# A redrawn order list and bank string for a fused delta-rule attention and MLP kernel

## The chip, the cores and the metric

The kernel runs on one core of one Trainium2 chip. The metric is the time of the device in microseconds (us), taken as the median of several runs. Each run starts the program once.

The core has five engines that run side by side, each through its own list of instructions: PE (matrix products, written to PSUM, which has eight banks of 128 x 512 float32), DVE and ACT (both read PSUM and SBUF; ACT also has the function tables), POOL (element work in SBUF, and the start of the weight transfers) and SP (starts of transfers). An engine executes its list strictly in order, and each instruction may wait for semaphores that other engines or transfers raise.

## The reference

The input is `q`, `k`, `v` of 4 batches x 8 heads x 768 positions x 48 dimensions, a factor `beta` for each position, and two weight matrices of 384 x 2048 and 2048 x 384. First comes a recurrence along the positions, then a dense block on its result:

```python
k_n = k / (norm(k) + 1e-6)
for t in range(S):                       # S = 768, one 48 x 48 state per head
    y[:, :, t] = einsum('bhd,bhde->bhe', q[:, :, t], state)
    v_old = einsum('bhde,bhd->bhe', state, k_n[:, :, t])
    state = state + b_t * einsum('bhd,bhe->bhde', k_n[:, :, t], v_t - v_old)
x = y, with the 8 heads x 48 side by side, 3072 rows of 384
h = x @ w_in
g = 0.5 * h * (1 + tanh(sqrt(2/pi) * (h + 0.044715 * h**3)))
out = g @ w_out
```

## The kernel before

**Chunks.** The recurrence is worked in 12 chunks (c0 to c11) of 64 positions for all 32 heads at once. Inside a chunk the dependence of one position on those before it is a triangular system; its inverse is built from 16 x 16 blocks: the small diagonal blocks are solved element by element (on DVE for c0, on POOL for c1 and for the later pairs c2/c3, c4/c5 and so on), and the larger block-triangular parts by Horner steps of matrix products (`inverse`, `factors`, `apply`). Chunks are then tied together by the state alone: `state(c)` computes R = K S - V, then U = T R, then the new state S from K and U, and the chunk's output x from S, Q, U.

**MLP.** When a chunk (c0 to c3) or a pair of chunks (from c4) has its x, `mlp` runs on these rows: the first product (m1, in units of one PSUM bank, each emptied by ACT with the gelu into `gT`), then the second (m2, eight tiles of `gT` at a time), whose result goes to `osb` and to DRAM. m1 needs all of `w_in` (six transfers on POOL, `g77` to `g82`), m2 the four parts of `w_out` (`g83` to `g86`). The MLP is the bulk of the PE's work and serves to fill its time between the short steps of the chunks.

**The order.** The program is first described as 1306 steps, numbered in the order in which the code makes them; each step says what it reads and writes, so its dependencies are known. A step is one or many instructions (a matrix step 2 to 64 products). Which engine runs a step, and in which order each engine runs its steps, is not computed: it stands written out in the string `ORDER`, where `p66` means "step 66 on PE", `v` is DVE, `a` ACT, `g` POOL and `s` SP (`a` and `s` also for transfers that these engines start). `w4.0` means four filler products of 512 columns into bank 0, which nobody reads. `BANK` gives for each PSUM tile the first of its banks. `Plan.schedule` (line 137) reads both, checks that no step stands ahead of one that it depends on, and makes a step that takes a bank wait for all users of the tile that had the bank before. `Plan.emit` (line 168) writes the five instruction lists with their waits. The position in `ORDER` matters only among steps of the same engine.

**Steps that the prediction names:**

| step | what it is |
|---|---|
| a23, a24 | masks mB0, mE0 (ACT) |
| 97, 99 | copy of the two halves of c0's transposed K out of PSUM into KQT (line 704) |
| 106, 107 | copy of the transposed Q of c0 and of c1 (line 673) |
| 112 | 1/norm of c1; 7, 49, 50, 51, 0: memsets (Kn, S3, the two EB halves, the filler's operand `wz`) |
| 75 | nbT, a transpose of beta (line 587); 71: bM of c0 |
| 158 to 180 | DVE's solve for c0 (177, 178: its last two large ops; 179, 180: into TB) |
| 187, 188 | c0's TT halves out of TB, four instructions each (line 934 on ACT, 935 on DVE) |
| 194, 196 ... 213 | PE steps of `apply` for c0, in two halves y = 0, 1 |
| 199, 201, 204, 207 | its results WB out of PSUM; 210, 214: U; 211, 215: the same for U3 |
| 217, 218, 219 | new state S after c0: product, copies S1 and S3 |
| 220 to 224 | output of c0: products, then copies into x |
| 135, 127 | K of c3 and c2; 136, 128: their transposes on PE; 137, 129: copies into KQT |
| 393, 394 ("own") | 64 small products each: diagonal blocks for c2 and c3; 396: their transpose Tt on DVE, which the POOL solve of c2/c3 starts from (397 to 426) |
| 316, 317 | for c1: K S on PE, and R on DVE (line 1162) |
| 312, 314; 313, 315 | c1's ET products and their copies |
| 318, 320, 322 ... 337 | PE steps of `apply` for c1; 319, 321: DI copies; 343 to 347: c1's output |
| 380, 381, 382, 383 | norms of c5 (square, sum) and of c4/c5 (square root) |
| 229, 231 ... 243 | m1 units of the first MLP tile; 230 ... 244: their gelu copies |
| 139, 140 | cast of Q for c2/c3 (POOL, ACT); 153 to 156: the loads of q for c4/c5, into the same buffer; 257, 258: casts of these; 259: transposes; 118 to 121: the loads of q for c2/c3 |
| 151, 152 | loads of k for c5 |
| 386, 389 | transposes of K for c4 and c5 |
| 443 | first Horner product of c2; 473, 474, 477, 478: c2's U product, its copy, and two products behind it |
| 1250, 1251 | last output product, last copy into x |
| 1298 to 1303 | the last m2 products; 1304, 1300: copies of their results into osb; 1293, 1297, 1305, 1301: transfers to DRAM |

Many DVE and ACT instructions are recorded under lines 252 and 257 (`f_tt`, `f_cp`) and 261 (`f_act`), PE's under 268 (`f_mms`) and transfers under 276 (`f_dma`), since these helpers make them.

## Time and profile before

| | us |
|---|---|
| median of 3 runs (lowest, highest) | 245.21 (243.59, 246.71) |
| the profiled execution, whole | 245.94 |
| its span from first to last instruction | 244.2 |
| PE busy in the span | 205.9 (84%) |
| DVE, ACT, POOL busy | 159.5, 154.4, 126.6 |
| instruction blocks (queue q8) | 35 transfers, 0.57 MB |

All times in the views are counted from the start of the span. The profiled execution took 1.7 us more than its span, and lies 0.7 us above the median. A busy time of PE counts a product from its issue to its modelled end, so neighbours overlap.

### The profile page before, as it was taken

How to read it: one execution, taken by the hardware profiler on the slowest of the kernel's cores; microseconds unless marked ns; L12 is line 12 of the kernel's file. 1: busy time of each engine (PE TensorE's matmuls, PEld its weight loads, DVE VectorE, ACT ScalarE, POOL GpSimd, SP SyncE). 2: the span in 40 equal slices, each digit the busy share in tenths (PEclk: the TensorE clock that was granted, in tenths of full speed). 3: DMA queues.
4: the chain of work that ended last, by engine and by line, in shares of the span. 5: the costliest groups of instructions: out<-in, count | busy, mean ns of one | idle time of the engine just before them, and what ended most of it. 6: DMA issues, size and time to landing. Idle time of an engine off the chain costs nothing.

```text
span 244.2 us, 10249 instructions
## 1 busy us (share of the span) xinstructions
PE 205.9 (84%) x4536; PEld 143.3 (59%) x4554; DVE 159.5 (65%) x300; ACT 154.4 (63%) x299; POOL 126.6 (52%) x267
## 2 busy tenths in 40 slices
PE   2144686498898889999998999999999799899995
PEld 2123565287755776877875666666566465555562
DVE  4689789459799979989799763893587453220000
ACT  0748635359699979973788979778631367105810
POOL 3566888189795886878504988358833000000000
PEclk9999999999999999999999999999999999999999
DMA  7979999795679247674435510044203202000122
GB/s 125 179 118 179 157 210 168 95 173 123 124 160 172 42 73 152 137 178 81 58 85 105 128 44 3 22 111 91 56 3 75 71 3 99 3 19 32 44 86 97
DMA packets 64780, 23.69 MB, mean 97 GB/s; under 512 B 53600, under 2 KB 63840, under 8 KB 64736
## 3 DMA queue, kind: packets, MB, share of 16 engines
q1 hardware_dynamic: 57984, 14.67, 34.7%
q0 software_dynamic: 1056, 3.15, 7.7%
q10 hardware_dynamic: 5696, 5.23, 7.1%
q8 instruction: 35, 0.57, 1.0%
q14 instruction: 9, 0.07, 0.1%
HBM read 20.64 MB, written 4.72 MB: 104 GB/s over the span
## 4 chain that ended last, share of the span: by engine, by line
PE 48%; DVE 18%; ACT 16%; DMA 7%; issue 5%; SPq 3%; ACTq 1%
PE ps L268 44%; SPq L276 3%; DMA x<-x 3%; DVE DT L752 2%; PE ps L697 2%; ACT KQT L261 2%; DMA qf<-in_q_dram 2%; DVE Tt L906 2%; DMA kf<-in_k_dram 2%; DVE EB L252 2%; ACT gT L261 2%; ACT EB L1099 1%; ACTq L276 1%; ACT Tt L736 1%; ACT x L261 1%
## 5 line engine op out<-in xcount | busy, mean ns | idle before, releaser
L268 PE MATMUL ps<-x,W 128*128 128x256 bf16 (+1 forms) x367 | 67.9, 325 | 5.0 <-DMA x<-x 2.1
L268 PE MATMUL ps<-W,gT 128*128 128x384 bf16 x384 | 66.8, 326 | 0.0
L261 ACT ACTIVATE gT<-ps 128x512 bf16<-128x512 f32 x96 | 53.0, 601 | 20.2 <-PE ps L268 19.5
L268 PEld LDWEIGHTS ps<-x,W 128*128 128x128 bf16 x384 | 39.2, 115 | 20.1 <-ACT gT L261 2.3
L268 PEld LDWEIGHTS ps<-W,gT 128*128 128x128 bf16 x384 | 35.9, 98 | 23.0
L795 POOL TENSOR_TENSOR Yf<-Yf,tmp 128x28 f32<-128x28 f32 (+13 forms) x84 | 30.1, 358 | 6.1
L252 DVE TENSOR_TENSOR TT<-ps,DI 128x768 bf16<-128x768 f32 (+2 forms) x30 | 20.6, 688 | 18.2 <-PE ps L268 18.0
L792 POOL TENSOR_TENSOR tmp<-Yf 128x28 f32<-128x28 f32 (+13 forms) x84 | 28.4, 338 | 6.0
L261 ACT ACTIVATE KQT<-ps 128x1024 bf16<-128x1024 bf16 (+1 forms) x16 | 15.5, 967 | 8.5 <-PE ps L697 6.8
L268 PE MATMUL ps<-KQT 48*64 48x128 bf16 (+1 forms) x640 | 12.7, 219 | 9.2 <-ACT KQT L261 5.7
L1029 POOL TENSOR_TENSOR DI<-TB,mB 128x384 bf16<-128x384 bf16 x14 | 13.0, 936 | 13.8 <-DVE TB L839 7.1
L261 ACT ACTIVATE osb<-ps 128x384 f32<-128x384 f32 x17 | 8.4, 493 | 17.9 <-PE ps L268 17.8
L257 DVE COPY osb<-ps 128x384 f32<-128x384 f32 x7 | 3.9, 551 | 24.1 <-PE ps L268 24.1
L752 DVE TENSOR_TENSOR DT<-ps,mD 128x512 bf16<-128x512 f32 x24 | 15.9, 680 | 2.7 <-ACT G L261 2.5
L268 PEld LDWEIGHTS ps<-KQT 48*64 48x64 bf16 (+1 forms) x640 | 9.2, 108 | 12.1 <-ACT KQT L261 7.2
L697 PE MATMUL ps<-identB,Kn 128*128 128x128 bf16 x96 | 8.9, 250 | 7.7 <-DVE Kn L252 6.0
L261 ACT ACTIVATE G<-ps 128x512 bf16<-128x512 f32 x24 | 13.9, 594 | 1.2 <-PE ps L268 0.8
L261 ACT ACTIVATE x<-ps 128x1024 bf16<-128x1024 f32 (+3 forms) x12 | 9.9, 829 | 7.2 <-PE ps L268 7.0
L261 ACT ACTIVATE U<-ps 128x768 bf16<-128x768 f32 (+1 forms) x9 | 7.0, 778 | 9.5 <-PE ps L268 9.5
L252 DVE TENSOR_TENSOR EB<-ps,mE 64x768 bf16<-64x768 f32 x13 | 12.3, 949 | 0.8 <-PE ps L268 0.5
L252 DVE TENSOR_TENSOR R<-ps,vf 128x768 bf16<-128x768 f32 x11 | 10.5, 952 | 3.0 <-PE ps L268 2.9
L252 DVE TENSOR_TENSOR S<-ps,S 128x768 bf16<-128x768 f32 x10 | 9.5, 951 | 4.4 <-PE ps L268 4.3
(144 smaller groups left out, 351.5 us busy)
## 6 DMA issues: line engine op xcount, KB each, us to landing
qf<-in_q_dram SPq DMA_DIRECT2D x24, 192.0 KB, 4.1
kf<-in_k_dram SPq DMA_DIRECT2D x23, 192.0 KB, 5.2
vf<-in_v_dram SPq DMA_DIRECT2D x40, 96.0 KB, 3.6
out_dram<-osb ACTq DMA_DIRECT2D x16, 192.0 KB, 1.9
W<-in_moe_w_out_dram POOLq DMA_DIRECT2D x4, 384.0 KB, 8.5
out_dram<-osb ACTq DMA_DIRECT2D x16, 96.0 KB, 2.8
vf<-in_v_dram SPq DMA_DIRECT2D x4, 192.0 KB, 5.7
W<-in_moe_w_in_dram POOLq DMA_DIRECT2D x2, 384.0 KB, 8.5
```

What stands on the lines that cost most here:

```text
L252: return lambda e: e.tensor_tensor(out() if callable(out) else out, a() if callable(a) else a, b() if callable(b) else b, op)
L257: return lambda e: e.tensor_copy(out, a() if callable(a) else a)
L261: return lambda e: e.activation(out, a() if callable(a) else a, func)
L268: ins = t.matmul(out, lhsT, rhs, start=st, stop=sp_, skip_group_check=skip)
L276: return lambda e: e.dma_start(out, a)
L697: ins = e.transpose(tb()[:, m, :], t[:, 2 * m:2 * m + 2, :].rearrange("p h d -> p (h d)"), identB[:, :])
L736: "act": lambda e: e.activation(X, gs_(0), ACT.Copy, scale=mH[:, 0:1]),
L752: op(d_ps(512), {"dve": lambda e: e.tensor_tensor(dv, gview(1)(), md, ALU.mult)}, reads=[h] + MD, writes=[dn])
L792: sop(nb * s * w, lambda e, s=s, w=w, tv=tv: e.tensor_tensor(tv, yf[:, :, s:s + 1, 0:s].to_broadcast([128, nb, w, s]), Yv()[:, :, s + 1:16 ...
L795: sop(nb * s * w, lambda e, s=s, tv=tv: e.tensor_tensor(Yv()[:, :, s + 1:16, 0:s], Yv()[:, :, s + 1:16, 0:s], tv, ALU.add), [YN, TN], [YN])
L906: op({"dve": 1.2 if early else 1.93}, {"dve": lambda e: e.transpose(Tt[j][:, 0:1024].rearrange("q (x y) -> q x y", y=32), own_view())}, re ...
L1029: return e.tensor_tensor(o_.rearrange("q p (b j) -> q p b j", j=16), i_.unsqueeze(2).to_broadcast([128, n_, 3, 16]), mB[:, 16 - 16 * w:64 ...
```

## The change

The string `ORDER` and the string `BANK` are replaced by others. The same 1306 steps are in it, each once, and the fillers are now `w6.3` (six products into bank 3) where `w4.0` stood elsewhere. No line of code outside the two strings changes: sizes, dependencies, loads and arithmetic are the same. 106 steps change their engine: 37 go from ACT to DVE and 36 from DVE to ACT, 10 from DVE to POOL and 8 from POOL to DVE, 13 transfers change between ACT and SP, one step goes from POOL to ACT and one back. DVE ends with 287 entries instead of 288, ACT with 310 instead of 312, POOL with 259 instead of 257, SP with 124 instead of 123, PE with the same 326. On every engine the order is another: at the start of the list the POOL's weight transfers `g77` to `g85` come earlier among its solve for c1, with `g86`, which stood first, after them; SP's loads are interleaved in another way; and PE runs the fillers ahead of step 393 rather than behind step 318. The diff, cut to the first 21 lines and the last two of each list, and the bank strings:

```diff
--- before.py
+++ after.py
@@ -17,68 +17,68 @@
 ORDER = """
-s54 v42 a55 g16 v1 v48 g21 v49 s52 g11 a53 s56 v46 v6 v47 v36 g12 g50 s57 g13 p66 g18 v68 v9 s59 v15 v3 v10 v37 v38
-v39 v5 v67 a87 g89 s63 v88 g17 v90 g19 v4 v40 v75 a2 s62 a91 a92 v93 s58 a108 v94 g95 s60 v41 p96 v69 s61 v109 g20 a97
-p98 s116 v72 v70 a28 v71 a99 a110 v0 p157 a111 v112 g113 v158 v159 g14 s145 p114 v161 s65 g22 v160 a115 g86 v162 v73
-v163 v164 g74 v43 v165 s117 v166 a27 p269 v167 a102 v168 v169 v170 a193 v171 s64 p104 v172 v173 v174 v270 a103 v175
-a25 g271 a33 p105 a29 a34 v176 v177 a106 g272 g273 a30 s146 a23 v178 a107 g274 g275 v8 v179 g276 a32 g277 p304 s101
-g278 v180 p181 g279 p184 g280 v188 a182 g281 s100 a26 g282 a185 v187 p196 g283 g77 a122 p191 v183 g84 a197 v45 v123
-p194 g284 p189 g285 a195 g286 a192 g83 v190 g85 a24 a305 p200 g80 p198 v201 g287 p205 g288 v199 p206 g289 v186 p202
-g290 p203 g291 v207 g292 p208 v204 g293 g294 v306 p209 g295 v76 g296 p212 g81 a210 p213 a124 a130 g297 v211 g298 v214
-g78 v131 p217 g79 p307 g35 v215 p220 g299 a132 a133 g300 a218 p221 g82 v134 v135 g395 a125 a308 p222 a219 v309 p316
-v126 v127 g301 p136 s151 p128 g302 v137 s152 v317 a129 g618 v303 a223 p393 g51 v310 a311 p394 a224 v216 a31 p318 a255
-v396 w4.0 v319 g397 v7 v256 p320 p314 g398 a321 g399 p312 g400 g401 p239 s120 v313 g402 s121 v315 g403 p322 s119 g404
-p326 p324 s118 g405 p329 v325 p243 g406 a380 s267 g407 g408 s268 a323 v381 g409 p235 g410 a382 p330 g411 a383 v384
-p233 g412 v331 p336 p337 g139 a244 p327 v338 a140 p241 v328 g413 v339 g414 a138 p141 v388 s153 a242 g385 p142 s155
-a236 p229 s156 v143 a234 s154 p332 a230 p333 v144 a240 g415 p343 v334 s391 p452 p344 v340 g416 a335 p436 s392 a453
-p345 g417 p346 a437 v454 g418 p347 a516 g419 v438 p386 g420 p237 a349 v348 g421 v387 a257 g422 p433 g258 p231 v517
-a434 g423 p259 s264 a238 v435 g424 p260 s149 a232 g425 p362 g426 s148 v261 g427 p455 s263 a363 v262 p389 s266 a456
-g575 v429 p598 p245 a599 v457 s431 a390 v600 s265 g428 v576 s150 a601 p608 p603 g819 s147 a609 v432 p250 a604 s430
-a610 v605 g459 v577 p251 v602 a606 a611 v607 g440 a458 v612 p613 g578 p364 v614 g518 s528 a439 p246 v615 s529 g519
-v619 a252 p443 a365 p368 a616 s225 v444 p462 g620 a369 s526 s226 p354 v44 v617 a445 s227 g621 v579 v441 g622 v580 s525
-a355 p446 g623 v581 s228 a463 v582 g624 v460 p356 g625 v447 g626 p341 a247 g627 v342 a464 p448 g628 p520 g629 v449
-p521 g630 a442 p465 v583 a522 g631 v584 p450 v585 g632 p471 v451 a357 a249 v586 g633 v466 a695 p366 g634 g587 v472
...
-a1261 p1258 p1276 a1259 p1141 a1273 a1285 a1265 p1266 a1142 p1270 a1143 p1274 a1267 a1271 p1288 a1275 p1302 a1283
-a1289 a1147 a1277 a1139 p1290 p1303 p1291 v1304 p1294 a1292 a1293 p1295 p1298 v1296 a1297 p1299 a1305 a1300 a1301
+s54 v51 a55 g13 g11 s52 v47 a53 v42 v37 v8 v48 g21 s56 g16 v43 v10 v1 v38 v36 v4 g17 s57 g14 g18 g12 v15 v39 p66 v68
+v9 s64 v44 v67 v3 v69 a87 g89 s58 g19 s61 v90 g20 v88 a2 s63 v40 v5 v6 a23 v72 a91 v41 a92 v70 s59 a108 v93 v94 g95
+s117 v109 p96 s60 g22 p98 v71 a24 a28 a110 v97 a111 v112 v7 v99 g113 v50 p157 s65 v45 v73 p114 g74 v158 v159 a115 s100
+a33 a32 v161 p269 s101 a30 a27 v160 a29 a102 v162 v163 v164 v165 s62 a25 a31 v166 p104 a34 a103 v167 v168 v169 v270
+a26 p105 s146 v170 g271 v171 v172 v173 v174 v175 s116 g272 v176 g84 v177 s145 g273 g81 v106 g82 v178 a107 p184 g274
+g78 v179 g80 a193 v75 g275 p304 a122 g276 v180 p181 g85 p307 v187 g277 g83 a308 g278 a182 v309 g279 a188 g280 v183 g77
+p194 g281 v76 p189 a195 g282 p196 g283 a185 v190 g284 v123 a197 p191 g285 a305 g79 p208 v186 p198 a124 g286 a130 g287
+v192 p202 g288 a125 a199 p200 g289 g290 p203 v201 g291 p205 g292 v204 p206 g293 v131 p209 g294 a207 g295 p212 g296
+v210 p213 g297 g298 v211 v126 a214 g299 v306 g86 a215 a132 p220 g300 a133 a255 g301 v134 p221 g302 v135 p222 g35 p217
+v256 g395 p136 v0 v127 g618 a137 v49 p128 s152 a218 s151 a224 w6.3 v219 a223 v303 a129 v216 a311 v310 p393 p394 p312
+s119 v396 s120 a313 s121 s118 g397 p316 s148 p314 v317 a380 s268 p243 g398 g399 v315 g400 s267 v381 g401 p318 g402
+g403 p241 a319 g404 g405 g406 p320 g407 p322 g408 a321 g139 p229 a382 v323 a383 v384 g409 g410 p329 g411 a244 p324
+g412 p235 v325 g413 v388 g414 p239 a236 a242 p330 g415 p389 a140 v331 g416 p237 g417 v390 s154 g418 p326 v385 a238
+p327 s155 g419 p336 p337 a240 s153 p141 v46 a230 s156 v338 p142 g420 a328 s391 v339 g421 p233 a138 v143 g422 s147 p386
+a234 v144 s392 p436 a516 p332 v387 p452 p333 a437 p343 v334 p344 v438 a335 a453 g258 p345 v340 p346 a257 g423 p347
+v454 p433 g424 s265 p231 g425 a434 v349 s263 g426 a348 g427 p259 v435 s264 a232 p260 v517 p362 a261 g428 p368 a363
+v262 p455 g575 a456 v429 p598 a369 v457 s431 a599 p603 v432 g440 s266 p608 a604 p250 s149 v609 a605 g459 v600 s150
+v610 a606 p251 s430 v458 g819 a601 v607 a611 s529 v602 g519 p364 a439 v612 p613 g518 v576 a365 p443 p462 a614 v577
+s226 p245 a444 g578 v615 s528 v579 v580 v619 g581 s228 a445 p246 g441 s225 g460 s526 a252 p446 a616 v582 s227 p356
+g620 v447 a357 v617 p341 a247 g621 v342 g622 a463 a254 p448 g623 p354 g624 v583 v449 g625 a464 p471 g626 v584 p450
+v472 g627 g628 a442 v451 g629 a695 p465 v585 p358 v586 v466 g587 a461 g630 p520 a588 a355 g631 p521 v589 a359 g632
...
+a1261 p1268 a1281 p1282 a1269 p1274 a1273 a1143 p1284 a1283 a1263 p1288 a1285 p1302 a1275 a1289 p1276 p1278 a1277
+p1290 a1279 a1151 a1139 p1298 p1294 p1291 p1295 v1292 p1303 v1296 a1297 p1299 a1304 a1293 a1305 a1300 a1301
 """
-BANK = ("0416354245051407147502621530774742261205463442577620577464266020462652544403457554231202235262300742"
-        "7670520665304776063065617606432407154221544705400200553433000264406526775135462326725256335252204005"
-        "42006200306737064473464535623002503636515011064657312544375303451726")
+BANK = ("0102013420246673452646262651747624063520570732466764745556360022552603452502542655432206626372770257"
+        "0742404667703365063000501545345737774237747451020210063462060250450227674374065547627457253252251006"
+        "70023110577231643650564272345225020336062300060571276745413307062135")
```

More of the change, by code (lines that the diff above doesn't have):

```diff
@@ new lines @@
+v590 p473 p477 g633 p467 v522 s596 g634 v474 a523 s597 g593 s527 v468 p478 p475 a479 a249 p591 g635 v476 p360 g636
+s488 v592 g637 p594 a361 g638 p469 s487 v696 a595 a485 g639 p530 s486 p799 g640 v470 p804 s351 v531 p366 a805 g641
+a484 g642 s352 p370 a776 v806 g643 s489 v800 g644 a367 g645 v801 s524 a807 p532 g646 v777 s525 p371 g647 a533 s353
+g648 g649 v778 a802 g651 v808 p536 a372 v803 p537 g650 a374 p814 v655 p809 p375 a538 v669 g779 v810 a815 v656 s544
+p376 a811 a253 v780 v816 s350 v652 a812 a817 p492 v670 s654 v781 v813 a377 g782 s653 p496 g697 a493 v818 s707 p490
@@ new lines @@
+a497 g657 v820 s708 p673 a491 p660 s548 p534 g658 a661 p502 s481 v535 p500 g821 a662 s483 v674 p504 s543 g822 a501
+a545 v783 s480 p663 v675 g823 g824 p498 a698 s547 v784 v664 p494 s546 g785 a672 g825 a499 a378 g826 p699 s482 g827
+p700 a495 g828 p665 a505 v701 g829 p511 a503 g830 v666 a896 g831 v786 v671 g832 p667 v702 a659 p682 g833 v668 p676
+g834 v683 p512 g835 v677 g836 s540 g837 p684 v787 a513 a248 s706 g838 v788 p555 g839 p678 g840 a556 p506 g841 v679
+a685 g842 v789 g843 v790 p686 g844 p507 v687 g845 g846 g847 v791 g848 p688 a508 p689 a510 p709 s798 g849 p680 g850
```

60 lines of the change are left out of this document (25 added, 35 removed).

## The prediction

> **What bounds the kernel now.** I read the page first, then busy time by stretch, the waits, the timelines of PE, DVE and ACT up to 66 us, and the traffic around one gap.
>
> ```profile
> span 244.2 us, 10249 instructions
> PE 205.9 (84%) x4536; PEld 143.3 (59%) x4554; DVE 159.5 (65%) x300; ACT 154.4 (63%) x299; POOL 126.6 (52%) x267
> q8 instruction: 35, 0.57, 1.0%
> 0.00:50.00 50.00, 24.69 (x721) 19.55 (x722) 36.74 (x102) 25.30 (x58) 30.82 (x71) 1.00 0.97 154
> 60.00:100.00 40.00, 35.63 (x892) 26.82 (x892) 35.48 (x64) 35.40 (x71) 31.30 (x61) 1.00 0.63 117
> 100.00:160.00 60.00, 58.16 (x1451) 42.06 (x1456) 47.94 (x80) 47.85 (x87) 37.79 (x81) 1.00 0.41 85
> 160.00:220.00 60.00, 56.74 (x1125) 35.27 (x1134) 30.53 (x39) 28.10 (x54) 17.82 (x38) 1.00 0.22 53
> 220.00:244.20 24.20, 21.23 (x116) 11.85 (x115) 1.11 (x2) 10.06 (x20) 0.00 (x0) 1.00 0.18 65
> ```
>
> The columns of the stretches are length, then busy time of PE, PEld, DVE, ACT, POOL, the granted clock, the DMA share and GB/s. PE is idle for 244.2 - 205.9 = 38.3 us, and 50 - 24.69 = 25.3 of that lies in the first 50 us, where x of the first chunks isn't there yet and the MLP can't fill. After it PE loses 4.4 (60 to 100), 1.8, 3.3 and 3.0 us. PE's work itself is the same in both lists (the same 326 steps), so only idle time can change: a list gains by shortening the head, or loses by drying PE out later.
>
> The head, with PE's own rows:
>
> ```profile
> 25.96 0.62 PE L268 MATMUL ps<-R,TT 64*64 64x48 bf16 x16 [0.67 <-DVE TT L935]
> 38.13 0.63 PE L268 MATMUL ps<-S,KQT 48*64 48x48 bf16 x32 [0.96 <-ACT osb L1214]
> 41.69 0.82 PE L268 MATMUL ps<-KQT 48*32 48x32 bf16 x80 [1.11 <-ACT KQT L261]
> 45.97 0.56 PE L268 MATMUL ps<-KQT 48*32 48x32 bf16 x48 [3.45 <-issue]
> 46.45 0.62 PE L268 MATMUL ps<-R,TT 64*64 64x48 bf16 x16
> 47.41 1.49 PE L417 MATMUL ps<-wz 128*128 128x512 bf16 x3 [0.33 <-issue]
> 50.82 0.43 PE L268 MATMUL ps<-DI,EB 64*64 64x48 bf16 x16
> 59.91 0.22 PE L268 MATMUL ps<-DT,U 64*64 64x64 bf16 x3
> ```
>
> These are, in turn, the first product of c0's `apply` (196), 316, step 393 with 16 products of 394, the rest of 394, 318, the fillers, 322 and 345. PE stops for 3.45 us in the middle of 394, at "issue": for nothing that is written in the list. The traffic from 36 to 42.4 us (first row) and from 42 to 46 us (second):
>
> ```profile
> q0 software_dynamic: 341, 1.10, 112.8%
> q8 instruction: 1, 0.02, 3.0%
> ```
>
> Until 42.4 the weight queue q0 holds all 16 engines and no instruction block is in the answer; one moves when it has thinned out. So I take the gap for a wait for PE's next block. A block is 0.57 MB / 35 = 16.3 KB, and 4536 + 4554 instructions over 35 to 36 blocks make some 256, that is 128 products with their loads. Counted back in the old list from 16 products into 394, 128 products reach the start of 316: the block was due to be asked for near 38.13 and was usable at 45.97, 7.85 us later, needed after 4.4.
>
> [...]
>
> **The change, part by part.** All of it is order, engine and bank. I follow the new list down the head with the durations of these rows:
>
> ```profile
> 12.45 0.69 DVE L252 TENSOR_TENSOR bM<-btz,mS 128x512 f32<-128x512 f32 x1
> 12.72 0.60 ACT L261 ACTIVATE KQT<-ps 128x512 bf16<-128x512 bf16 x1
> 25.07 1.70 DVE L935 TENSOR_SCALAR TT<-TB,mBs 128x128 bf16<-128x128 bf16 x8
> 34.03 0.56 DVE L257 CAST U<-ps 128x384 bf16<-128x384 f32 x1
> 38.30 1.00 DVE L252 TENSOR_TENSOR Kn<-kf,rn 128x768 bf16<-128x768 f32 x1
> 40.37 0.95 DVE L252 TENSOR_TENSOR R<-ps,vf 128x768 bf16<-128x768 f32 x1
> 46.60 1.25 DVE L906 STREAM_TRANSPOSE Tt<-ps 128x1024 f32<-128x1024 f32 x1 [3.19 <-PE ps L268]
> L257 DVE COPY KQT<-ps 128x1024 bf16<-128x1024 bf16 x9 | 6.1, 681 | 1.0 <-PE ps L697 0.5 <-PE ps L665 0.3
> L480 POOL MEMSET EB<- 128x512 f32 x2 | 1.0, 517 | 0.0
> L587 DVE STREAM_TRANSPOSE nbT<-gT 128x192 f32<-128x192 f32 x1 | 0.5, 489 | 0.0
> L257 DVE CAST WB<-ps 128x384 bf16<-128x384 f32 x7 | 3.7, 543 | 1.5 <-PE ps L268 1.5
> ```
>
> *Loss before c0's `apply`.* Copies 97 and 99 go from ACT to DVE, behind bM, which ends at 13.14. A half copy on DVE isn't in the trace; it lies between half of the 681 ns of a whole one and ACT's 0.60, and I take 0.4, nearer the same engine's row. With 112 and memset 7 between them, 99 ends near 14.2 rather than 13.32: +0.9. The EB memset (50) that follows, 0.52 us on POOL, lies under the products that 99 releases; without that cover it would cost its 0.5. Copy 106 now stands between 177 and 178 in DVE's solve (+0.6 of its 0.68), nbT (75) between 179 and 180 (+0.4 of its 0.49). Together +1.9: first product near 27.9.
>
> *Gain inside it.* 188 goes to ACT, beside 187 on DVE, where eight instructions took 1.70 us in series; two of DVE's four WB copies (543 ns) go to ACT, beside the other two. I put that at 0.5 for TT and 1.0 for WB, so U is complete at 34.59 + 1.9 - 1.5 = 35.0, 0.4 later than now. DVE's steps from there to K of c2 (127) are the same but for wz's memset and one square sum in place of others; K ends near 39.5 (now 39.30).
>
> *394 and the block.* Behind 136 and 128 (40.4) PE runs six fillers; three took 1.49, so six take 2.6 to 3.0, and 393 starts at 43.0 (now 41.69): 1.3 lost. By the same count of 128 the block that 394 needs falls due 42 products into it instead of 16, and is asked for at the start of 136, near 37.7: needed 6.4 us later instead of 4.4. Of the weights, the last is now started by POOL at
>
> ```profile
> 36.32 0.55 POOL L276 DMA_DIRECT2D W<-in_moe_w_in_dram  x1
> ```
>
> The new list has nine of the ten started before step 286 of its solve and so some 4 us ahead of now; only 86 stays near 37. So q0 should thin out some 4 us earlier, near 39 instead of 42.4 to 45. I take the 3.45 as gone; 394 ends at 44.5 (now 46.53). If the block again takes 7.85, 1.5 is left.
>
> *A new order on DVE.* R of c1 (317) now stands behind Tt (396), which waits for 394; now it runs at 40.37, before 394. New: 44.5 + 1.25 + 0.95 + waits = 47.1, and who waits for it is 318: 47.1 against 46.45, +0.65. But no fillers follow 318; 312 and 314 are done, and one m1 unit stands there. 322 comes at 48.7 against 50.82: -2.1. Step 345 I put at 57.2 against 59.91.
>
> *The q buffer.* What releases the second MLP tile and the solve of c2/c3:
>
> ```profile
> 52.19 0.94 DVE L613 TENSOR_REDUCE ss<-sq 128x16 f32<-128x768 f32 x1
> 53.67 1.28 ACT L261 ACT_TABLE_LOAD   x1
> 55.46 0.84 ACT L261 ACTIVATE Qn<-qf 128x768 bf16<-128x768 f32 x1
> 57.74 5.77 DMA qf<-in_q_dram
> 63.53 0.84 ACT L261 ACTIVATE Qn<-qf 128x768 bf16<-128x768 f32 x1 [1.41 <-DMA qf<-in_q_dram]
> ```
>
> Sum 381 (52.19) stands in the new list right behind 315 and so ends near 48.5 to 49.1 (the later if the loads 151 and 152 of k for c5 take as long as now), against 53.13. Root, table load and three gelu copies follow, then cast 140: done at 52.7 to 53.3 against 56.30. The next q is loaded behind it; with the 7.2 us from there to 63.53 the cast 257 starts near 60.2 instead of 63.53: -3.3. I take 3.0 for the head as a whole, between 2.1 and 3.6.
>
> *The rest of the list.* By 343 the new list has done two more transposes (389, 386) and one more m1 unit, by 443 it has as much less, so this evens out. For each PE step behind I counted the PE work listed between the product that feeds a copy and the reader of that copy. Both lists leave the same few places thin (around 473, where a reader of U or of its bank stands one or two steps behind) and cover the others. So I put the body at nothing, with 2 us either way from its 4.4 us of idle time in 60 to 100. The tail:
>
> ```profile
> 209.88 0.34 PE L268 MATMUL ps<-KQT,S 48*48 48x64 bf16 x21 [0.92 <-issue]
> 241.32 0.49 ACT L261 ACTIVATE osb<-ps 128x384 f32<-128x384 f32 x1 [4.71 <-PE ps L268]
> 241.84 0.34 ACTq L276 DMA_DIRECT2D out_dram<-osb  x1
> ```
>
> On ACT the last copy (1300) now stands behind 1304 and the starts 1293 and 1305; 1304 reads the product before the last, so the starts (0.34 or more each) may push 1300 by up to 0.4. The second block wait (0.92) may stay, go or move.
>
> Sum: 245.94 - 3.0 + 0.4 = 243.3 for an execution like the profiled one, and 0.7 less for the median: **242.6 us**.
>
> **Rivals.** (A) *The gap stays once.* The block again comes only when q0 lets it, or the gap at 42.5 has another cause that stays with 394: 394 ends 3.45 later, 317 and 318 with it, and 322 at 52.1 against 50.82; the later gains are used up. Against it: the list starts the weights earlier. For it: the last one, 86, starts as late as the last one now (36.32). Time 245.2 (244 to 247). [...]
>
> (B) *The head gains and PE dries out less behind it.* Of 4.4 us in 60 to 100 half goes, since q and k come 3 us earlier, and the 0.92 too: 245.2 - 3.0 - 2.2 - 0.9 = 239.1 (237 to 240.3).
>
> (C) *Slower: two blocks fall due inside the weight stream.* One block earlier the boundary lies at 206, with 128 products from there to 136, about 4.3 us. If a block takes 7.85 us from its boundary wherever q0 is full, PE waits 3.5 us before the transposes of K and again 3.45 in 394: 245.2 - 3.0 + 7.0 = 249.2 (247 to 251). It decides once both boundaries are passed before q0 thins out. For it: the stream starts earlier, 206 lies inside it. Against it: now the same boundary (in 209) is passed under the stream without a stop.
>
> **How the numbers follow.** Forecast 0.45, own range 240.3 to 245; A 0.19, B 0.24, C 0.12. About 2%, 4.9 us, is what a measurement of this kernel can tell from no change. Faster by over 2% means under 240.3: B and a fifth of the forecast, 0.33. Slower, over 250.1: a part of C and what I haven't seen, 0.09. The rest, 0.58, lies within. The range from 237 to 248 takes in A, B and the forecast's bounds and leaves out most of C.
>
> **What would show it.** In the profile after: 196's product near 27.9; no "issue" gap over 1 us in the PE rows between 36 and 48 (A: one of 3 us in 394, C: one before the transposes as well); R of c1 behind Tt, 318 near 47, 322 near 49; cast 257 near 60; PE busy in 60 to 100 within 2 us of 35.6. The prediction is wrong if 257 doesn't come earlier, or if it does and PE loses it again before 160.

## The result and the profile after

The changed kernel takes 241.94 us (241.59 to 242.01, 4 runs), the kernel before beside it 245.35 us (243.59 to 246.71): a ratio of 0.989, 95% interval 0.984 to 0.994. By the 2% line that is no change; the gain of 1.1% is nevertheless clear of zero. A later comparison gave 242.23 us and 0.989 again (0.984 to 0.994). Ratios leave out the executions more than 1.5% above the fastest of the same kernel, so a ratio can differ a little from the quotient of two medians.

The profiled execution of the changed kernel took 241.95 us, its span 240.2. Its page, and busy time by stretch in the columns that the prediction explains; the last fence is the one stretch of the profile before that the sums below need and that has not been shown:

```profile
span 240.2 us, 10275 instructions
PE 207.0 (86%) x4539; PEld 143.9 (60%) x4556; DVE 158.4 (66%) x297; ACT 157.7 (66%) x309; POOL 130.2 (54%) x269
```

```profile
0.00:50.00 50.00, 26.83 (x716) 20.32 (x718) 38.34 (x103) 26.48 (x61) 30.40 (x71) 0.98 1.13 168
50.00:60.00 10.00, 10.00 (x239) 8.25 (x241) 7.64 (x13) 7.97 (x17) 8.67 (x20) 0.95 0.51 98
60.00:100.00 40.00, 35.73 (x1027) 27.76 (x1013) 38.41 (x67) 34.08 (x69) 32.21 (x62) 1.00 0.62 120
100.00:160.00 60.00, 58.32 (x1328) 41.06 (x1332) 46.14 (x75) 46.06 (x84) 40.41 (x80) 1.00 0.38 79
160.00:220.00 60.00, 58.88 (x1165) 36.81 (x1174) 26.72 (x39) 34.59 (x66) 18.48 (x39) 1.00 0.21 53
```

```profile
50.00:60.00 10.00, 9.41 (x251) 7.77 (x248) 7.69 (x15) 7.69 (x15) 8.90 (x19) 1.00 0.82 144
```

PE is idle for 240.2 - 207.0 = 33.2 us instead of 38.3. Up to 60 us the idle time is 23.2 (was 25.9), from 60 to 160 it is 6.0 (was 6.2), from 160 to 220 it is 1.1 (was 3.3). So a gain appears in the head, as forecast, and a second one behind 160 us, which was not. These sums are rough: 17 or 18 of the products have no record in either profile (x4539 against x4556 loads here), and a product is busy for longer where PE ran slower (in this profile a group of six took 1.47 us at a granted clock of 0.50 and 0.84 us at 1.00, see the fillers below), so idle time is not the whole of what a list can change. The head in PE's own rows:

```profile
28.65 0.62 PE L268 MATMUL ps<-R,TT 64*64 64x48 bf16 x16 [1.42 <-DVE DT L752]
39.49 0.24 PE L268 MATMUL ps<-U,Kn 64*48 64x48 bf16 x2 [1.16 <-issue]
42.22 2.20 PE L417 MATMUL ps<-wz 128*128 128x512 bf16 x5 [0.67 <-ACT KQT L261]
44.34 1.21 PE L268 MATMUL ps<-KQT 48*32 48x32 bf16 x128
46.90 0.44 PE L268 MATMUL ps<-S,KQT 48*64 48x48 bf16 x32 [0.98 <-ACT EB L952]
48.91 0.62 PE L268 MATMUL ps<-R,TT 64*64 64x48 bf16 x16
51.17 0.41 PE L268 MATMUL ps<-DI,EB 64*64 64x48 bf16 x16
61.12 0.22 PE L268 MATMUL ps<-DT,U 64*64 64x64 bf16 x3 [0.16 <-PE ps L268]
```

They are the first product of c0's `apply` (194, 196), the end of 217, the fillers, 393 and 394 as one piece, 316, 318, 322 and 345. The stop of 3.45 us in 394 is gone; one of 1.16 us stands two products ahead of the end of 217. ACT's rows for what releases the second tile, with the cast 257 last:

```profile
51.37 0.49 ACT L261 ACTIVATE DI<-ps 128x384 bf16<-128x384 f32 x1 [1.30 <-PE ps L268]
52.26 1.28 ACT L261 ACT_TABLE_LOAD   x1
62.33 0.85 ACT L261 ACTIVATE Qn<-qf 128x768 bf16<-128x768 f32 x1 [0.91 <-DMA qf<-in_q_dram]
```

### The profile page after: what moved, and what is told of

Its sections match the earlier page's. It is cut to its first block, busy times and chain, and to the rows that moved or that the text cites. A ratio compares the mean times of both kernels' runs of the same rounds, so it can differ in the third digit from the quotient of the medians.

```text
span 240.2 us, 10275 instructions
## 1 busy us (share of the span) xinstructions
PE 207.0 (86%) x4539; PEld 143.9 (60%) x4556; DVE 158.4 (66%) x297; ACT 157.7 (66%) x309; POOL 130.2 (54%) x269
## 4 chain that ended last, share of the span: by engine, by line
PE 61%; DVE 19%; ACT 8%; DMA 4%; issue 3%; POOL 2%; SPq 1%; ACTq 0%
PE ps L268 58%; DMA kf<-in_k_dram 2%; DMA qf<-in_q_dram 2%; ACT KQT L261 2%; DVE DT L752 2%; PE ps L697 2%; DVE WB L1029 2%; DVE ss L613 2%; POOL Kn L252 1%; ACT G L261 1%; ACT gT L261 1%; DVE TT L252 1%; DVE Tt L744 1%; PE ps L417 1%; DVE TB L839 1%
## 5 line engine op out<-in xcount | busy, mean ns | idle before, releaser
L268 PEld LDWEIGHTS ps<-x,W 128*128 128x128 bf16 x384 | 40.0, 115 | 17.2 <-DVE S L252 0.6
L257 DVE COPY osb<-ps 128x384 f32<-128x384 f32 x9 | 4.9, 555 | 30.3 <-PE ps L268 30.3
L261 ACT ACTIVATE KQT<-ps 128x1024 bf16<-128x1024 bf16 x12 | 12.3, 1026 | 13.1 <-PE ps L697 6.8
L261 ACT ACTIVATE osb<-ps 128x384 f32<-128x384 f32 x15 | 7.4, 491 | 18.1 <-PE ps L268 17.5
L1029 POOL TENSOR_TENSOR DI<-TB,mB 128x384 bf16<-128x384 bf16 x16 | 15.0, 954 | 7.4 <-DVE TB L839 4.0
L268 PE MATMUL ps<-KQT 48*64 48x128 bf16 (+1 forms) x640 | 12.1, 217 | 7.0 <-DVE KQT L257 4.4
L261 ACT ACTIVATE x<-ps 128x1024 bf16<-128x1024 f32 (+3 forms) x15 | 12.0, 807 | 9.4 <-PE ps L268 9.1
L1099 ACT ACTIVATE EB<-ps,mE 64x256 bf16<-64x256 f32 x36 | 14.3, 462 | 4.0 <-PE ps L268 1.7
L613 DVE TENSOR_REDUCE ss<-sq 128x16 f32<-128x768 f32 (+1 forms) x13 | 11.4, 882 | 1.1 <-POOL sq L252 1.1
```

The costliest lines, as they stand in the source:

```text
L257: return lambda e: e.tensor_copy(out, a() if callable(a) else a)
L261: return lambda e: e.activation(out, a() if callable(a) else a, func)
L268: ins = t.matmul(out, lhsT, rhs, start=st, stop=sp_, skip_group_check=skip)
L613: fr = lambda e, u=u: e.tensor_reduce(ss[j][:, u], sq[:, u, :], AX.X, ALU.add)
L1029: return e.tensor_tensor(o_.rearrange("q p (b j) -> q p b j", j=16), i_.unsqueeze(2).to_broadcast([128, n_, 3, 16]), mB[:, 16 - 16 * w:64 ...
L1099: ins = e.activation(eb[:, :, :, cc], view(h, 48, 8, g)()[rr, :, :, cc], ACT.Copy, scale=mE[rr, 16 * b:16 * b + 1])
```

## The experiments

The kernel before scatters between 242.7 and 248.6 us over all comparisons, so every ratio below is against its runs beside the same kernels, with a 95% interval.

### Weights early in the old list

POOL's ten weight transfers take the places that they have in the new list; every other step of the old list stays.

```diff
-... g282 g283 g77 g84 g284 g285 g286 g83 g85 g80 g287 ... g296 g81 g297 g298 g78 g79 ...
+... g271 g272 g84 g273 g81 g82 g274 g78 g80 g275 g276 g85 g277 g83 ... g280 g77 ... g285 g79 ... g299 g86 ...
```

> The old list, in which only POOL's ten weight transfers (77 to 86) stand at the places that they have in the new list among its solve for c1; nothing else moves. Theory (the weight stream holds up PE's instruction block): the stop of 3.45 us in the middle of step 394 goes or falls below 1.2 us, step 394 ends near 43.5 instead of 46.53, and the idle time of PE in the first 60 us falls by 2 to 3 us; the time comes down to 242.5 to 244 if what follows keeps it. Rival (the stop belongs to step 394, or is set by how many instructions lie behind it): the 3.45 us stay at the same product and the time is that of the old list, 245.3 within 0.8.

253.4 us (249.3 to 254.8), ratio 1.029 (1.018 to 1.039): slower, where neither the theory nor its rival had it. PE's rows and, from the chain of waits, the transfer behind them:

```profile
33.89 0.57 PE L268 MATMUL ps<-WB,EB 64*64 64x48 bf16 x14 [1.35 <-issue]
46.33 0.26 PE L268 MATMUL ps<-DT,U 64*64 64x64 bf16 x3 [9.10 <-DVE x L257]
52.09 1.25 PE L268 MATMUL ps<-KQT 48*32 48x32 bf16 x128 [1.11 <-ACT KQT L261]
```

```profile
22.63 21.64 DMA kf<-in_k_dram
```

Two things follow. The stop in 394 is gone (393 and 394 run as one piece of 128), and one of 1.35 us has come up in `apply` of c0. And the last of k's loads before the gap, which starts at 22.63 us, right behind the first of these weights (22.41), lands after 21.6 us: DVE waits for the squares of that k, and PE behind it for 9.1 us. The new list starts k's loads 100 and 101 earlier as well, the last of them at 19.53, ahead of every weight; I take that for the reason why it can start the weights early, but no run moves these loads alone.

### The two halves apart

The lists hold nearly the same steps in their first 540 entries (89 us) and in their first 1020 (161 us), so one can be cut and the other put behind it. `BANK` is cut with the list: no run moves it alone.

```diff
-ORDER = old list
+ORDER = first 540 entries of the new list, then the rest in the old order (first run)
+ORDER = first 1020 entries of the old list, then the rest in the new order (second run)
+ORDER = first 540 entries of the old list, then the rest in the new order (third run)
```

> The new list for its first 540 entries (about the first 89 us), then the remaining steps in the old list's order and on its engines. Theory (two separate gains: 2.7 us less idle time of PE up to 60 us, and some 2 us in 160 to 220 from the x copies): this kernel keeps the first alone, 242.3 to 243.5, and shows the waits for x near 190 and 217 and the stop of 0.9 again. Rival 1 (the head's gain is given back later, the whole comes from 160 to 220): 244.8 to 245.8. Rival 2 (the whole comes from the head, the waits for x go by themselves when the head is early): 241.5 to 242.2.

> The old list for its first 1020 entries (about the first 161 us), then the remaining steps as in the new list. Theory of two gains: idle time of PE in 160 to 220 falls from 3.3 to about 1.2 us with the head as before, 242.8 to 243.9. Rival 1 (all from the end): 241.6 to 242.4. Rival 2 (all from the head): 244.8 to 245.8.

> The old list for its first 540 entries (about the first 89 us), then the remaining steps as in the new list. It answers to the run with the new list up to there and the old one behind, which showed 245.7 us median against 244.5 for the old list. Theory 1 (the head is worth under 1 us, the gain of the new list is made behind 89 us): 241.5 to 243, within 1 us of the new list. Theory 2 (the gain is made in the head): 244 to 245.5.

New head alone: 245.7 us, ratio 1.004 (0.999 to 1.008). New end alone: 243.7, 0.997 (0.993 to 1.001). Old head with all the rest new: 243.1, 0.991 (0.987 to 0.996). By the times the larger part of the gain is made behind 89 us, and the head by itself shows none. The first run lies where rival 1 has it, the second within its theory's range, the third just above theory 1's.

The traces say how constant the rest is. From the end of step 530 (near 90 us) to the end of the span I get, from PE's step ends:

| kernel | 530 ends | from there to the end |
|---|---|---|
| before | 91.05 | 153.2 |
| new head, old rest | 89.64 | 152.9 |
| old list, x transfers shared out (below) | 89.29 | 152.1 |
| old to 161 us, new end | 90.37 | 151.5 |
| old to 89 us, new rest | 90.93 | 151.8 |
| changed kernel, two profiles | 88.26, 88.01 | 151.9, 152.1 |

The new rest is worth some 1.1 us (152.9 and 153.2 with the old rest, 151.5 to 152.1 with the new). The head differs from profile to profile with the same steps in it: 89.3 to 91.05 with the old one, 88.0 to 89.6 with the new.

### The x transfers

In the old list, six small transfers complete the x of the last tile but one; five are started by ACT, one by SP. In the new list ACT starts four and SP two; ACT's stand apart, with its copies between them, and no osb transfer is among them. The first run here shares them out three and three.

```diff
 (old list)
-a1103 s1100 a1099 s1087 ... a1098 a1101 ... a771 ... a1102
+s1103 a1099 s1100 a1101 s1098 a1102 s1087 ... a771
```

> The old list, in which only the six small transfers that complete the x of the last tile but one (1098 to 1103) are shared out anew: three on SP and three on ACT instead of one and five, ahead of a transfer of osb on ACT and of the last load of v on SP. Theory (PE's waits for DMA x near 192 are these starts queued on ACT): the waits of 1.2 us at the products and 1.1 us at the weight loads there go, and the time falls by 1.2 to 2.3 us, to 243.0 to 244.2. Rival (what PE gains there is waited for at the next place, the m1 units behind, whose banks ACT's gelu copies release): under 0.6 us is left, 244.7 to 245.4.

243.4 us, ratio 0.998 (0.994 to 1.002): by the times, not to be told from no change. By the trace, the wait near 190 us went. ACT's starts in the kernel before, PE's wait there, and in the third fence ACT's and SP's starts in the changed kernel:

```profile
185.66 2.46 ACTq L276 DMA_DIRECT2D x<-x  x4
188.16 0.59 ACTq L276 DMA_DIRECT2D out_dram<-osb  x1
188.78 0.51 ACTq L276 DMA_DIRECT2D x<-x  x1
```

```profile
192.63 0.59 PE L268 MATMUL ps<-x,W 128*128 128x512 bf16 x2 [1.24 <-DMA x<-x]
```

```profile
182.70 0.52 ACTq L276 DMA_DIRECT2D x<-x  x1
183.24 1.26 SPq L276 DMA_DIRECT2D x<-x  x2
186.00 0.51 ACTq L276 DMA_DIRECT2D x<-x  x1
186.55 1.33 ACTq L276 DMA_DIRECT2D x<-x  x1
187.91 0.61 ACTq L276 DMA_DIRECT2D x<-x  x1
```

A start costs ACT about 0.6 us (one row of the changed kernel reads 1.33), and in the old list four stand in a row; the last of the old list is started 3.1 us after the first, and its landing ends PE's wait of 1.24 us. The changed kernel has no wait for x there, although its last start comes 5.2 us after its first; the new head with the old rest has it again (1.21 us at 192.13). The other way round, the six starts of the new list are put in a row and shared out as in the old one:

```diff
 (new list)
-s1103 ... a1099 s1098 ... a1100 ... a1102 a1101
+a1103 s1100 a1099 a1098 a1101 a1102
```

> The new list, in which the six small transfers 1098 to 1103 are shared out as in the old list, five on ACT in a row and one on SP, instead of three and three. Theory (the share-out of these starts is the gain of the new list behind 160 us): PE waits again for DMA x near 190, by 0.6 to 1.5 us, and the time is 0.6 to 1.5 us above the new list's, 0.990 to 0.995 of the old list. Rival (the new list has enough PE work ahead of the first product that needs the transfers, so the share-out alone changes nothing there): no wait for x over 0.3 us, time within 0.5 us of the new list, 0.986 to 0.991.

244.5 us, ratio 0.994 (0.991 to 0.998), against 0.989 (0.984 to 0.994) for the new list: in the theory's range, though the intervals overlap. The place of the wait was another than either expectation had. ACT's rows, then PE's:

```profile
184.90 3.21 ACTq L276 DMA_DIRECT2D x<-x  x5
188.16 3.63 ACT L1099 ACTIVATE EB<-ps,mE 64x256 bf16<-64x256 f32 x9 [2.90 <-DVE WB L1029]
```

```profile
189.40 0.44 PE L268 MATMUL ps<-S,KQT 48*64 48x48 bf16 x32 [1.28 <-ACT EB L1099]
```

No product waits for x. The five starts hold ACT for 3.2 us, the copies into EB come behind them, and PE waits 1.28 us for EB. From step 530 to the end this run took 153.4 us, 1.3 to 1.5 more than the new list. So in the profiles the place and share-out of these six starts account for the gain of 1.1 us behind 90 us, from both sides; the times alone show half a per cent for it in this run and nothing clear of noise in the first. A stop at issue of 1.44 us at 90.17 us, just ahead of the end of 530, adds to this profile's span.

### Where PE stops: blocks and the weight stream

Counting PE's product records from the start of the program, every stop at issue over 0.5 us up to 66 us of all profiles stands at one of a few places, 125 to 130 products apart or a multiple of that:

```
list                          stops: products before it (us)
old (four profiles)           606 (3.45, 1.88, 1.32, 2.19); 988 (0.60)
old, weights early            350 (1.35)
old, 40 products put ahead    606 (1.95)
new (two profiles)            476 (1.16, 1.41)
new, no fillers; x as in old  476 (1.41); 476 (1.41)
new head, old rest            476 (1.41), 731 (0.77)
new, weights late             476 (0.87), 730 (0.98)
old, w_out late               732 (1.18)
new, w_out late               730 (1.74), 857 (0.81), 984 (2.56)
```

That the stops wait for blocks can be read directly, since the trace lists every packet of the instruction queue q8, one block of 16 KB each. Over the whole spans of the 14 profiles there are 26 stops at issue of over 0.5 us, and every one ends 1.3 to 1.8 us after such a packet has arrived. In the profile before, the packet moves from 42.49 to 44.41 us and the stop in 394 ends at 45.97. Counted back from the first stop of a profile in steps of 128 weight loads, the first six packets of the profile before (up to 52.62 us) start 1.1 to 4.4 us behind such a boundary, the first fifteen of the profile after (up to 100.09 us) 0.35 to 3.7 us behind; further on this count drifts and some packets start ahead of it. So there a packet follows a boundary, as the prediction took it; what sets the packet off is not shown. Seven of the 26 lie behind 66 us, where no weights move, among them the 0.92 at 209.88 in the profile before and the 1.44 at 90.17 in the run above.

The changed kernel once more, to see the chance in it:

```diff
 (no edit: the changed kernel)
```

> The changed kernel once more, beside the three that follow. The kernel before has come out between 242.7 and 247.7 us so far, and in three profiles in which the old list ran its first 161 us or all of it, the stop in the middle of step 394 was 3.45, 1.88 and 1.32 us long. Theory (part of the scatter and of the 3.45 is chance in when the block of instructions comes, and the new list has only a smaller stop of 1.2 to 1.4 us in step 217): the new list's own times lie closer together, within 1 us of 242, and the stop in 217 shows again with 0.8 to 1.6 us. Rival (the first four executions lay close by chance): they spread over 3 us or more, and the median lies at 242 to 243.5.

242.23 us (240.72 to 244.21): the rival was right on the scatter (3.5 us, not 1), the theory on the stop (1.41 us in 217). The old list's 3.45 us belonged to one profile; in three others, with the same steps up to there, the stop was 1.3 to 2.2.

The next kernel moves the boundary by 40 products, and with them only the memset of their operand:

```diff
-s54 v42 a55 ... p66 g18 v68 ... v72 v70 a28 v71 a99 a110 v0 p157
+s54 v0 v42 a55 ... p66 w40.1 g18 v68 ... v72 v70 a28 v71 a99 a110 p157
-                    ins = e.matmul(psum[:, b, :], wz[:, 0:128], wz[:, :], start=True, stop=True)
+                    w = 512 if n < 10 else 64
+                    ins = e.matmul(psum[:, b, 0:w], wz[:, 0:128], wz[:, 0:w], start=True, stop=True)
```

> The old list with 40 more filler products of 64 columns, which nobody reads, right behind step 66 on PE, where PE is idle from about 5 to 11 us; the memset of their operand moves to the head of DVE's list. Nothing else changes: every later product is 40 places further on in PE's list. Theory (PE stops where one block of 256 instructions ends): the stop leaves the 17th product of step 394 and comes 40 products earlier in the work, at the 41st of step 393, still at the same place counted from the start of PE's list (product 606 of 4594), or it is hidden there by the wait for KQT, in which case the other stops stand at 478, 734 or 988 in the same count. Rival (the stop belongs to step 394 and what it needs): it stays at the 17th product of 394. The time is within 2 us of the old list in both.

PE's rows:

```profile
41.28 0.49 PE L268 MATMUL ps<-KQT 48*32 48x32 bf16 x40 [1.11 <-ACT KQT L261]
43.72 0.91 PE L268 MATMUL ps<-KQT 48*32 48x32 bf16 x88 [1.95 <-issue]
```

The stop left 394 and stands behind 40 products of 393, again at product 606 of the list, as the theory had it. So the stop goes by the count of products, not by the step. The time, 246.6 us (ratio 1.008, 1.003 to 1.012), is above the old list: 530 ended at 89.3, but the profile lost time behind it, with a new wait of 1.94 us for ACT at 151.5 us and a granted clock of 0.50 for the 3.4 us behind that, where 16 products took 4.45 us and the next 16 of the kind 2.77. How forty products that nobody reads come to move waits that lie 110 us later is not shown.

What makes the block late is asked by moving the weight stream, first all of it, then w_out alone:

```diff
 (new list, weights late: POOL's weights as in the old list)
-... g272 g84 g273 g81 g82 g274 g78 g80 ...
+... g283 g77 g84 g284 ... g286 g83 g85 g80 g287 ...
 (w_out late, on the old and on the new list)
-g83, g84, g85, g86 among 271 to 299
+g402 g83 ... g404 g84 ... g406 g85 ... g409 g86
-               reads=WAFT,
+               reads=[],
```

> The new list, in which only POOL's ten weight transfers (77 to 86) stand at the places that they have in the old list among its solve for c1. Theory (the weight stream sets where PE waits for its block): the stop in step 217 near 38.3 goes or is below 0.5 us, and one of 1.3 us or more comes back within step 394, as in the old list; the time is 0 to 2 us above the new list's. Rival (the new list's order of the other engines, not the weights, took the stop out of 394): no stop over 1 us in 394, the one in 217 stays.

> The old list, in which the four transfers of w_out (83 to 86, 1.5 of the 2.7 MB that the weight queue carries) start behind steps 402, 404, 406 and 409 of POOL's next solve, near 51 to 54 us, instead of among the solve for c1; they are also freed of the gate that ties them to the first loads of q, without which the next loads of q would wait for them. In the runs so far the time from one block boundary of PE to the product behind the next was 5.7 to 7.9 us wherever PE waited under the weight stream. Theory (the block is held up by the weight stream): with less than half of the stream left, the stop in step 394 falls below 0.8 us, and the loads of k for c2 and of q for c2/c3 land earlier; the time falls by 1 to 2.5 us. Rival 1 (the block takes 6 us or more whatever else moves): the stop in 394 stays over 1.3 us and the time within 1 us of the old list. Rival 2 (w_out now meets the loads of q and k near 55 us): the stop goes, but the cast 257 starts later than 64 and the time is that of the old list or above.

> The same edit on the new list: w_out behind steps 402, 404, 406 and 409. Theory (weight stream): the stop in step 217, 0.9 to 1.4 us in five profiles, falls below 0.5, and the time by 0.3 to 1.5 us against the new list (0.984 to 0.988 of the old). Rival 1 (block time fixed): stop stays, time within 0.5 us of the new list. Rival 2 (w_out collides later with q): 1 us or more above the new list.

Weights late in the new list: 242.6 us, ratio 0.990 (0.985 to 0.995), the new list's time. PE's rows:

```profile
39.02 0.23 PE L268 MATMUL ps<-U,Kn 64*48 64x48 bf16 x2 [0.87 <-issue]
...
50.98 0.24 PE L268 MATMUL ps<-R,TT 64*64 64x48 bf16 x5 [0.98 <-issue]
```

The rival holds: with the old weight times no stop comes back in 394. With w_out late the old list takes 246.4 us (1.008, 1.003 to 1.012), the new one 248.2 (1.016, 1.010 to 1.021). The stops in 394 and in 217 are gone, and in the new list three others stand one block apart under the shifted transfers; the second fence is the weight queue's traffic from 48 to 66 us there, where the changed kernel has none:

```profile
51.87 0.24 PE L268 MATMUL ps<-R,TT 64*64 64x48 bf16 x5 [1.74 <-issue]
58.76 0.83 PE L665 MATMUL ps<-identB,Qn 128*128 128x128 bf16 x12 [0.81 <-issue]
65.49 0.21 PE L268 MATMUL ps<-DT,x 64*64 64x64 bf16 x1 [2.56 <-issue]
```

```profile
q0 software_dynamic: 576, 1.57, 49.6%
```

So the stops move with the transfers, but they do not need the weights. Between the boundary and the block's packet, the engines were full of loads of q, k and v alone ahead of the first of the three stops above (queue q1, 114.7% from 45.4 to 49.1 us), and so they were ahead of the stop at 50.98 in the run with late weights (110.1% from 45.2 to 47.9). On the time rival 2 of both expectations holds; 257 starts at 63.9 us in the old list (forecast: later than 64, before: 63.53) and at 66.25 in the new one (62.33 in the changed kernel).

### The fillers

```diff
 (new list)
-... s151 a224 w6.3 v219 a223 ...
+... s151 a224 v219 a223 ...
```

> The new list without its six filler products (w6.3, which nobody reads). In the changed kernel's chain of waits they stand with 2.2 us (42.22 to 44.41) ahead of step 393. Theory 1 (the six are on the path that sets the end): step 393 starts near 42.2 instead of 44.3 and the time falls by 1 to 2 us, to 240 to 241. Theory 2 (what follows waits for something else: the instruction block, or R of c1 behind Tt): 393 starts earlier but a stop at issue or another wait takes its place, and the time is that of the new list within 0.6 us. Theory 3 (without them PE's granted clock falls): the clock in the 10 us behind is below the 0.88 to 1.00 seen so far.

244.0 us, ratio 0.997 (0.993 to 1.000): about 0.8% above the new list (the intervals just overlap), against theories 1 and 2. Without the fillers (first fence) and with them, in the second profile of the changed kernel:

```profile
45.25 1.25 PE L268 MATMUL ps<-KQT 48*32 48x32 bf16 x128 [2.57 <-ACT KQT L261]
...
49.01 1.46 PE L268 MATMUL ps<-x,W 128*128 128x256 bf16 x6
50.96 1.41 PE L268 MATMUL ps<-x,W 128*128 128x256 bf16 x6
```

```profile
43.12 1.62 PE L417 MATMUL ps<-wz 128*128 128x512 bf16 x5 [0.66 <-ACT KQT L261]
...
48.30 0.85 PE L268 MATMUL ps<-x,W 128*128 128x256 bf16 x6
49.56 0.85 PE L268 MATMUL ps<-x,W 128*128 128x256 bf16 x6
```

393 has to wait for ACT's copy of KQT with or without them: the fillers fill a wait. What they buy in this pair of profiles is speed: the same six products take 1.46 us without them and 0.85 with them. Step 345 ends 2.0 us later without them (63.1 against 61.1). The column of the granted clock reads 1.00 in both, but for want of an entry: the trace's list of clock periods begins, with full speed, only at 52.19 us in the run without fillers, where such a group takes 0.85 us from 53.07 on, and at 43.87 in the second profile of the changed kernel. So without them PE stays slow for longer, which is theory 3 by its effect, and the sign is that first entry: 43.9 to 46.0 us in the six profiles with the fillers ahead of 393, 48.4 to 51.3 in the old list's four and in the one with 40 products ahead. By one run the stop in 394 has a part in the late entry: with w_out late, which takes that stop away, it comes at 45.55 in the old list. Where the list has entries the column shows them; these are stretches of the first profile of the changed kernel, in which the group took 1.47 us at 47.52 and 49.47 and 0.84 at 51.51:

```profile
47.56:50.97 3.41, 3.41 (x34) 2.04 (x34) 2.24 (x3) 0.51 (x2) 2.78 (x9) 0.50 1.22 182
50.97:54.38 3.41, 3.41 (x76) 2.90 (x78) 2.37 (x4) 2.95 (x6) 3.10 (x7) 1.00 0.28 36
```

The traces show two speeds, 1.72 to 1 for this group (1.46 against 0.85 us). But for the last one of each trace, cut off by its end, the periods in the lists of the profiles before and after are 3.41 us long or whole multiples of that: 194.56 us before; 3.41, 3.41 and 191.15 us after. What makes the speed fall is not shown: PE was busy for 2.43 of the 3.41 us ahead of the fall at 47.56, and in the second profile it was busy for 2.47 of 3.41 us (from 43.87) and kept full speed.

No kernel tried beats the changed one.

## Why the prediction was right in its number and wrong in much of its sum

**Sum and forecast.** 242.6 us was forecast; 241.94 and 242.23 were measured, within the forecast case's own range of 240.3 to 245. Of the signs that were named, PE's busy time in 60 to 100 us came as said and 257 came earlier; one gap at issue over 1 us stands between 36 and 48 us (1.16), and 196, 318, 322 and 257 were all later than put. Against the profiled execution before, 245.94, the terms were -3.0 for the head, nothing for the body, +0.4 for the tail. That execution lay high: all comparisons put the old list's median at 244.5 to 245.8.

**Loss before `apply`.** Forecast 27.9 for its first product, measured 28.65: +2.7 instead of +1.9. The sum had DVE's solve and left out that the last wait is for DT, another DVE step behind it (1.42 us).

**Gain inside it, K of c2.** The gain was put at 1.5 and is 1.4, but behind the larger loss: U was put at 35.0 and is complete at 35.9 (DVE's half ends at 35.29, ACT's, started at 35.42, at 35.91), 1.3 later than before. K of c2 was put at 39.5 and ends at 39.84, which held.

**394 and the block.** The stop went, and 394 ends at 45.6 (forecast 44.5). The position, 42 products into 394, was counted rightly (128 products behind the stop at 476 it is 40), and that a count of products sets the place held as well, as the shift by 40 products shows (606 in both). The reason given, weights started 4 us earlier, was not what took it away: with late weights it is gone too. Nor did q0 thin out near 39: from 39.5 to 41.8 us its packets took 101.4% of the 16 engines' time. By these runs what counts is the work between two boundaries against the time of a block, 5.7 to 7.9 us at the stops under the weight stream. The old list needs the block 4.4 us after the boundary; in the new list the next need, at product 604, came 5.6 us after the stop at 476, and the block's packet had arrived by 42.75, 2.3 us ahead of it. So the term "needed 6.4 us later instead of 4.4" was the one that carried the step. One boundary earlier, in 217, the new list stops for 1.16 us: rival C's first place, at a third of its 3.5. What it costs is open: it lies on the chain of waits that ended last, since the first transposes behind it (136) need only K of c3, which is ready at 37.89; but in the new list with w_out late, where it is gone, 393 starts at 44.55, no earlier than here. Of the 35 or 36 blocks of a profile one to three end with a stop of over 0.5 us; PE passes the others without one.

**R behind Tt.** This step failed first. 318 was put at 47.1 and starts at 48.91, 322 at 48.7 and starts at 51.17: not earlier than before (50.82). 345 was put at 57.2 and starts at 61.12, 1.2 later than before. Of the 1.8 us at 318, 1.1 are 394's. Most of the rest is a wait that the sum left out: R of c1 reads the product 316, and in the new `BANK` 316 takes bank 3 behind 312, so it has to wait until ACT has copied 312's result into EB (0.98 us of PE at 46.90; the second profile has the same 0.98 at 47.68). DVE ends Tt at 46.90 and can start R only at 47.52. In the old list 316 stood ahead of all this, at 38.13, in another bank. Behind it, the two groups of products ahead of 318 and 320 ran 1.47 instead of 0.85 us, at a granted clock of 0.50 from 47.56 to 50.97, in this profile; in the second they ran 0.85, and 322 starts at 50.7.

**The q buffer.** This step failed with it. 257 was to start at 60.2 and starts at 62.33, 1.2 earlier than before instead of 3.3. I let root and table load follow the sum 381 directly. In the new list ACT first has the copy 321 of a product of c1's `apply` (51.37, after a wait of 1.30 for PE), and the table load stands behind it at 52.26. So the delay of R went through ACT into q, which the prediction had taken to be free of it.

**The fillers.** The sum had them as a loss: 393 put at 43.0 for 41.69. It starts at 44.34, but ACT's copy of KQT ends at 44.14, so the fillers are not what holds it. What they do for the speed of the groups behind them, the run without them shows (1.46 against 0.85 us), and the sum had no term for it: it held PE's work to be the same in both lists.

**The body.** Forecast: nothing, within 2 us. From 60 to 100 us PE's busy time is 35.73 (was 35.63), as said. But the change of 13 transfers between ACT and SP was named in the list of changes and never costed, and one of them, the share-out of 1098 to 1103, is worth, in the profiles, the 1.1 us behind 90 us. The row that would have told it, the wait of 1.24 us for x at 192.63, stood in the trace of before.

**The tail.** +0.4 forecast; from the last copy's start to the end of the span it is 2.9 us in both. Nothing lost. The stop of 0.92 at 209.88 went.

**The size of the head.** It was put at 3.0. The changed kernel's two profiles end it (step 530) 1.0 to 3.0 us ahead of the old list's four, and without its share-out of the x transfers the new list still gains (0.994, 0.991 to 0.998); but with the old rest behind it the times show no gain (1.004), and its profile ends 530 at 89.6, within the old list's 89.3 to 91.05. How much of the head's lead the median keeps stays open: the stop in 394 alone varies by 2.1 us between profiles of the same steps. So the number came out right with steps of the head that failed and a term that was missing (the x transfers), and that these came near to cancelling is luck.

## What to carry to other kernels

Before a stop is costed from one profile, see whether it has the same length in another: here a stop of 3.45 us was 1.3 to 2.2 in three others. When transfers change their engine, cost the starts as instructions of that engine: about 0.6 us each here, and five in a row held ACT for 3.2 us ahead of its copies into EB. Where PE stops at issue, count its products: here the stops lay 125 to 130 products apart or a multiple of that, 40 products put ahead moved one from 394 to 393, and with w_out late the ones in 394 and 217 went while others came up further on. Before a product is moved behind another, look at which bank it gets and whose copy has to empty it (0.98 us of PE at 316 here).

## What the runs showed of the hardware

Every stop of PE at issue of over 0.5 us in 14 profiles, 26 in all, ended 1.3 to 1.8 us after a 16 KB packet of the instruction queue had arrived. From the crossing of one boundary to the first product behind the next it took 5.7 to 7.9 us at the stops under the weight stream, and still 3.2 us at the stop at 59.48 us in the run with three x transfers on each engine, where the packet started 0.35 us after the crossing. One transfer of k of 192 KB landed after 21.6 us behind early weights, against a median of 5.2 us in the profile before. The column of the granted clock reads 1.00 where the trace has no clock entry yet, so ahead of the first entry the durations of a repeated group are the sign (1.46 against 0.85 us). And the first entry came at 52.19 us without the six fillers and at 43.9 to 46.0 with them.
